# One transpose copy moved to ScalarE, the bias transpose planned later, new tie noise: a planned FFT-filter-and-MLP kernel on one core

## The chip, the core and the metric

One core of a Trainium2 chip runs the whole program. The metric is device time in microseconds (us) of one execution; a run's number is the median of several executions. Engines are named as in the profile: PE (TensorE) multiplies, PEld loads its weights, DVE is VectorE, ACT is ScalarE, POOL is GpSimd, SP is SyncE, which issues most DMAs.

## The reference, cut to what is computed

`x` is 2048 tokens of 512 values. A spectral branch filters it with a 2-D FFT, a dense branch is an MLP with the activation `h * tanh(softplus(h))` (Mish), and a gate per token mixes them.

```python
x = A_x                                                    # (1, 2048, 512) bf16
g = sigmoid((x * gate_w).sum(-1, keepdims=True))
a = irfft2(rfft2(x) * (A_w_r + 1j * A_w_i), s=(2048, 512)) # (2048, 257) filter
h = x @ B_w1 + B_b1                                        # 512 -> 1792
sp = log1p(exp(-abs(h))) + where(h > 0, h, 0)
b = (h * tanh(sp)) @ B_w2                                  # 1792 -> 512
return g * a + (1 - g) * b
```

## The kernel before, in words

**Tasks and a planner.** The kernel does not write its instruction order down. `_build` records 603 tasks with `G.add` and its wrappers (`pe`, `evict`, `tt`, `dma`; lines 449 to 487): each has an engine, a guessed duration, what it reads and writes, the banks of PSUM it needs and a priority. `_Graph.schedule` (line 203) then plays the program through with the guessed durations. At every step it takes the tasks that could start within 0.03 us of the earliest one and picks the one with the highest priority (lines 271 to 278). For loads the guess of when the data is there is a table, `LAND` (line 355). To each priority a small random number is added: `NOISE` times a draw from `SEED`, and for every number in `MORE` another 2% of the tasks draw again (lines 217 to 222). So ties, and near ties, are settled by the noise. What comes out is one fixed order per engine; the chip runs each engine's list strictly in that order, and a task waits on semaphores for those it depends on. Nothing is reordered at run time. Banks of PSUM are handed out by the planner too: a task that needs a bank waits for the one that last emptied it.

**Tiling.** Tokens are 16 tiles of 128. In what follows a task's name is that of the code:

- `tr0` to `tr3` (one tile each), `tr4`, `tr6` ... `tr14` (two each): PE transposes of x into PSUM, four 128x128 matmuls a tile (line 559). `evx0` ... copies the result to `xT` in SBUF (line 563, executed at lines 480 on DVE and 481 on ACT). Which engines may take a copy is said at line 565: tiles 8 to 15 DVE or ACT, the others DVE alone.
- The dense branch goes in four chunks of 512 tokens. `mm1_c_f` is chunk c times block f of 14 blocks of w1's columns: four matmuls of 128x512 into one bank (line 901). The first four blocks of chunk 0 are split into halves `a` and `b` of four 128x256 matmuls, since w1's rows land in two parts. `mish_c_f` (ACT, line 915) adds the bias `b1f` and applies Mish; it empties the bank. `mm2_t_0` and `mm2_t_1` are the two halves, seven matmuls each, of the second product for token tile t (line 932); `bev_t` (ACT, line 881) scales the result by 1-g for tiles 0 to 13, and `fin_14_1`, `fin_15_0` and `fin_15_1` (DVE, line 944) finish the last two.
- The bias: `ld_b1` loads b1 as 14 rows (ACT's DMA queue, line 529), `tr_small` turns it with one PE transpose (line 568), `ev_small` (DVE, line 571) writes `b1f`. Every `mish` needs it.
- The spectral branch, forward: `ts`/`td` add and subtract halves of `xT` (line 485, two of them on POOL); `a10_t`, `a11_t` (PE, line 597) are DFTs along the 512 values; `eg_t` (ACT, line 604) and `e1p_t`, `e1m_t`, `e1f_t` (DVE or ACT) combine them; `s1_t` (PE, line 628) is a first stage along the tokens; `e2_t` empties it and `r1w`/`r1r` DMAs reshape through memory. Then `s2_v0` (PE, line 736), the filter products `wm` (DVE, line 485, 128x1024) and `wz` (POOL, line 485, 128x510), and `s2i_v` (PE, line 819) back, with `e4` and a second pass through memory (`r2w`, `r2r`). A small side path corrects columns 0 and 256: `s2c` (PE, line 726), `cvec` (DVE, line 752), `crv` (POOL, lines 757 and 758), `rcc` (PE, lines 765 and 766), `cvec2`, `cm`, `chs`, `z0`.
- The spectral branch, last stage, per token tile t: `s1i_t` (PE, line 848), `e5_t` (DVE or ACT, lines 480 and 481), `a1i_t` (PE, line 860, into bank 5 or 6), `gc_t` (ACT, line 865), `sap_t` and `sam_t` (DVE, line 871), `sbp_t` and `sbm_t` (POOL, a few on DVE), and `sum_t` (DVE, line 485, 128x512), which adds the dense result before the store.
- The gate: `gdot_t` (DVE), `gpow` (POOL), then `gadd1` (line 655), `gcol1` (line 657) and `omg1` (line 658) on DVE for tiles 4 to 15.

Dense and spectral PE work has no order of its own but the data's: the planner fills the waits of the spectral chain with dense blocks. Before the first transposes PE runs 36 warm-up matmuls on constants (line 505).

The copy's options and the bias transpose, the places that the change touches:

```python
engs=("dve", "act") if t0 in EVA else ("dve",)             # EVA = (8, 10, 12, 14)
...
pe("tr_small", 0.1, ..., reads=["braw", "ident"], writes=["ptb"], alloc=pb)
```

Of the kernel before, what the change touches and what calls it, by code (L numbers as in the profile page):

```python
# [152 lines left out]
class _Graph:  # L153
# [49 lines left out]
    def schedule(self):  # L203
# [28 lines left out]
        while left:  # L232
# [100 lines left out]
S1N = 2  # L333
S1B = [(6, 7), (4, 5), (2, 3)]
A1B = (3, 4, 5)
SEED = 655
NOISE = 0.02
MORE = (875162, 119001, 117053, 53775, 256917, 33723, 661048, 937753, 617580, 523774, 550536, 317180, 864218, 698349, 47742, 135651, 44963, 55085, 378986, 311594, 322092, 969305, 898997, 781312, 307590, 286182, 632606)
SPEC = (3, 4, 5, 6, 7)
DENSE = {0: (0, 1), 1: (0, 1), 2: (0, 1, 7), 3: (0, 1, 7)}  # L340
DENSE2 = {0: (0, 1), 1: (0, 1), 2: (0, 1, 2, 7), 3: (0, 1, 2, 7)}
# [5 lines left out]
EVA = (8, 10, 12, 14)  # L347
GDD = 0
JOIN = 0
GD_N = 4  # L350
FOLDP = ('d2', 'd3')
P2B = ((2, 3), (4, 5))
PAIR = (0, 1, 2, 3)
COLD = 3.9
LAND = dict(ld_x0=3.0, ld_x1=3.2, ld_x2=4.0, ld_x3=4.3, ld_w1_a0=4.9, ld_w1_a1=5.1,
            ld_b1=6.3, ld_fd=6.3, ld_w1_b0=5.7, ld_w1_b1=6.1, ld_x4=9.0, ld_x6=9.2,
            ld_w1_4_0=10.0, ld_w1_4_1=10.6, ld_x8=12.0, ld_x12=13.6, ld_w1_8_0=14.4,
            ld_w1_8_1=15.1, ld_m10=16.6, ld_m11=17.9, ld_w1_12_0=18.4, ld_w1_12_1=18.8, ld_gw=19.2, ld_sm=19.5,
            ld_w2_0=22.0, ld_w2_1=24.4, ld_gd=24.8)
PR = dict(tr=99.0, sp=95.0, mm1=88.0, mish=97.0, mm2=70.0, fin=98.0, gate=96.9, sum=98.5)  # L360


def _build(nc, A_x, A_w_r, A_w_i, B_x, B_w1, B_b1, B_w2, gate_w, out):
# [6 lines left out]
    G = _Graph()  # L370
    es = ExitStack()
    with es:
# [4 lines left out]
        xT = sb("xT", [128, 4, NT * 128], BF)  # L377
        Tg = sb("Tg", [128, 8192], BF)
        act = sb("act", [128, 3, NFT, 512], BF)
# [5 lines left out]
        sm = sb("sm", [128, 320], BF)  # L385
# [31 lines left out]
        In2 = Abuf[:, 0:8192].rearrange("p (u g k) -> p u g k", u=8, g=4)  # L417
# [58 lines left out]
        def pe(name, dur, fn, **kw):  # L476
            return G.add(name, "pe", dur, fn, lat=0.17, **kw)
# [6 lines left out]
        def tt(name, o, i0, i1, op, n, rate=1.0, engs=("dve",), lock=True, **kw):  # L484
# [8 lines left out]
              reads=["ones"], writes=["ident"])  # L493
# [58 lines left out]
        for t0, w in ((0, 1), (1, 1), (2, 1), (3, 1), (4, 2), (6, 2), (8, 2), (10, 2), (12, 2), (14, 2)):  # L552
            pt = _Ps(SPEC[::-1])
            def f_tr(e, t0=t0, w=w, pt=pt):
                ins = None
                for i in range(w):
                    for c in range(4):
                        o, d0 = (c * w + i) * 128, 256 * (c // 2) + c % 2
                        ins = e.transpose(psb[:, pt.bank, o:o + 128], xo[:, t0 + i, d0:d0 + 255:2], ident[:, :])  # L559
                return ins  # L560

            pe(f"tr{t0}", 4 * w * mm(128), f_tr, reads=[("x", t0 + i) for i in range(w)] + ["ident"], writes=[("ptr", t0)], alloc=pt, prio=PR["tr"] + max(0, 4 - t0) * 0.2)
            evict(f"evx{t0}", 512 * w, lambda t0=t0, w=w: xT[:, :, 128 * t0:128 * (t0 + w)],
                  lambda pt=pt, w=w: psb[:, pt.bank, 0:512 * w].rearrange("p (c j) -> p c j", c=4), rate=2.0,
                  reads=[("ptr", t0)], writes=[("xT", t0 + i) for i in range(w)], frees=[pt], engs=("dve", "act") if t0 in EVA else ("dve",), prio=PR["tr"] + max(0, 4 - t0) * 0.2)
            if t0 == 3:
                pb = _Ps(SPEC[::-1])
                pe("tr_small", 0.1, lambda e, pb=pb: e.transpose(psb[:, pb.bank, 0:14].rearrange("p (a b) -> p a b", b=2), braw[0:14, :],
                                                                    ident[0:14, :].rearrange("p (b a) -> p a b", b=2)[:, 0:7, :]),
                   reads=["braw", "ident"], writes=["ptb"], alloc=pb)  # L570
                G.add("ev_small", "dve", 0.2, lambda e, pb=pb: e.tensor_copy(out=b1f[:, :], in_=psb[:, pb.bank, 0:14]),
                      reads=["ptb", "b1t"], writes=["b1f"], frees=[pb])
# [165 lines left out]
            return ins  # L738

        p2_01 = [[_Ps(P2B) for _ in range(2)] for _ in range(2)]  # L740
        if JOIN:

            def f_s2j(e):
                f_s2c(e)
                return f_s2(e, (0, 1), 2, p2_01[1])

            t_s20 = pe("s2_00", 2 * mm(512), lambda e: f_s2(e, (0, 1), 0, p2_01[0]), reads=[("In2", r, i) for r in range(2) for i in range(2)] + ["sm"],
                       writes=[("p2", 0, c) for c in range(2)], alloc=p2_01[0], prio=PR["sp"] + 1.6)
            pe("s2_cj", 0.03 + 2 * mm(512), f_s2j, reads=[("In2", r, u) for r in range(2) for u in range(8)] + ["sm"], writes=["pc", ("p2", 1, 0), ("p2", 1, 1)], alloc=[pc] + p2_01[1], deps=[t_s20], prio=PR["sp"] + 1.6)
        else:  # L750
            pe("s2c", 0.1, f_s2c, reads=[("In2", r, u) for r in range(2) for u in range(8)] + ["sm"], writes=["pc"], alloc=pc)
        G.add("cvec", "dve", 0.3, lambda e: e.tensor_copy(out=cvec[:, 0:2, :].rearrange("p c (r u) -> p r c u", r=2),
                                                          in_=ps[:, pc.bank:pc.bank + 2, 0:16].rearrange("p r (c u) -> p r c u", c=2)),
              reads=["pc"], writes=["cvec"], frees=[pc])
# [26 lines left out]
        for v in range(4):  # L781
            u0, zb = 2 * v, v % 2
            q_of = {}
            p2s = p2_01[v] if v < 2 and JOIN else [_Ps(P2B) for _ in range(2)]


            for cs in (((0, 1),) if v in PAIR else ((0,), (1,))):
                if v < 2 and JOIN:
                    continue
                pe(f"s2_{v}{cs[0]}", len(cs) * mm(512), lambda e, f=f_s2, cs=cs, u0=u0, p2s=p2s: f(e, cs, u0, p2s), reads=[("In2", r, u0 + i) for r in range(2) for i in range(2)] + ["sm"],  # L790
                   writes=[("p2", v, c) for c in cs], alloc=[p2s[c] for c in cs], deps=s2is[v - 2:v - 1] if v >= 2 else ())
            for c in range(2):
                p2 = p2s[c]
                for i in ((0, 1) if c == 0 else (1, 0)):
                    s = nq % 5
                    nq += 1
                    q_of[c, i] = s
                    tt(f"wm{v}{c}{i}", lambda s=s: Qb[:, s],
                       lambda p2=p2: ps[:, p2.bank:p2.bank + 2, :].rearrange("p r (u k) -> p r u k", u=2),
                       lambda i=i, u0=u0: WT[:, i, :, 0:256].rearrange("p (r u) k -> p r u k", r=2)[:, :, u0:u0 + 2, :],  # L800
                       ALU.mult, 1024, lock=False, reads=[("p2", v, c)] + WALL, writes=[("Q", s)], frees=[p2])
            for (c, k0, k1, op) in ((0, (0, 0), (1, 1), ALU.subtract), (1, (0, 1), (1, 0), ALU.add)):
                s0, s1 = q_of[k0], q_of[k1]
                for rho in range(2):
                    tt(f"wz{v}{c}{rho}", lambda zb=zb, c=c, rho=rho: Zb[:, zb, rho, c, :, 1:256],
                       lambda s0=s0, rho=rho: Qb[:, s0, rho, :, 1:256], lambda s1=s1, rho=rho: Qb[:, s1, rho, :, 1:256], op, 510,
                       engs=("pool",), reads=[("Q", s0), ("Q", s1)], writes=[("Z", zb, rho, c)])
            G.add(f"wc{v}", "pool", 0.2, lambda e, zb=zb, u0=u0: e.tensor_copy(
                out=Zb[:, zb, :, :, :, 0], in_=z0[:].rearrange("p c (r u) -> p r c u", r=2)[:, :, :, u0:u0 + 2]),
                reads=["z0"], writes=[("Z", zb, 2)], lock=True)  # L810
            p3 = _Ps([(4, 5, 6, 7)])

            def f_s2i(e, zb=zb, p3=p3):
                ins = None
                for c in range(2):
                    for rho in range(2):
                        for g in range(4):
                            r = slice(32 * g, 32 * g + 32)
                            ins = e.matmul(ps[64 * rho:64 * rho + 64, p3.bank + g, :], RI[r, c, :],  # L819
                                           Zb[r, zb, rho, c].rearrange("p u k -> p (u k)"), start=(c == 0), stop=(c == 1))  # L820
                return ins

            t_s2i = pe(f"s2i_{v}", 2 * mm(512) + 0.04, f_s2i, reads=[("Z", zb, 2)] + [("Z", zb, r, c) for c in range(2) for r in range(2)] + ["sm"],
               writes=[("p3", v)], alloc=p3)
            s2is.append(t_s2i)
            for g2 in range(2):
                evict(f"e4_{v}{g2}", 1024, lambda u0=u0, g2=g2: T2s[:, u0:u0 + 2, 2 * g2:2 * g2 + 2, :].rearrange("p u g k -> p g u k"),
                      lambda p3=p3, g2=g2: ps[:, p3.bank + 2 * g2:p3.bank + 2 * g2 + 2, :].rearrange("p g (u k) -> p g u k", u=2),
                      reads=[("p3", v)] + S1R, writes=[("T2s", v, g2)], frees=[p3])
            dma(f"r2w{v}", scr2_w[:, 8 * v:8 * v + 8, :], T2s[:, u0:u0 + 2].rearrange("p u g k -> p (u g) k"),  # L830
                reads=[("T2s", v, 0), ("T2s", v, 1)], writes=[("scr2", v)], nbytes=128 * 4096, tail=0.5)
# [235 lines left out]
```

## Time and profile before

| | before |
|---|---|
| median of 3 runs | 131.83 us (131.78 to 131.84) |
| the profiled execution, its own time | 131.52 us |
| its span, first to last instruction | 129.8 us |
| TensorE clock granted | 1.00 |
| PE busy | 126.1 us, 97% of the span |
| DVE, ACT, POOL busy | 90.5, 73.4, 62.8 us |

Busy time is the time in which an engine executed; a row of the timeline gives its start, its length, engine, line, operation and tiles (out<-in) and how many instructions of the kind it merges; in brackets stands idle time of that engine ahead of it, with what ended it. The ends of PE's matmuls are modelled, so two PE rows may overlap by some tenths; starts are what counts.

### The profile page before, as it was taken

Reading aid. Unit: us, or ns where it says so; the run is one execution under the profiler, and the core shown is the slowest. Engines: PE = TensorE matmul, PEld = TensorE weight load, DVE = VectorE, ACT = ScalarE, POOL = GpSimd, SP = SyncE. Lnnn points to the kernel's source line nnn. Section 1 sums busy time; section 2 is a strip of 40 time slices with the busy share of each in tenths; the row PEclk is TensorE's granted clock in tenths of the full one; section 3 lists DMA queues with packets and bytes.
Section 4 is the critical chain, followed back from the end, with each engine's and each line's share of the span. In section 5 each row is a group of like instructions: output and inputs, shape, how many; then the busy total and the mean of one; then the engine's idle time right before and its main releaser. Section 6 shows DMA issues by size and latency. Waiting matters only on the chain. (4 is left out here: it accounts for less than half of the span.)

```text
span 129.8 us, 2596 instructions
## 1 busy us (share of the span) xinstructions
PE 126.1 (97%) x983; PEld 67.0 (52%) x983; DVE 90.5 (70%) x166; ACT 73.4 (57%) x120; POOL 62.8 (48%) x90
## 2 busy tenths in 40 slices
PE   7899999999999999999999999999999999999992
PEld 7787756454544443433343434344566555545452
DVE  0538989997669978978694863300267998999672
ACT  0456779755642776768678688804357374362230
POOL 3000143993536025976979094000019689579700
PEclk9999999999999999999999999999999999999999
DMA  3999999699995494800410503156910022222024
GB/s 93 304 355 400 384 343 333 203 221 228 204 319 167 94 374 188 323 5 0 127 37 0 162 5 107 54 162 197 408 47 3 0 86 81 81 83 81 0 87 160
DMA packets 15929, 21.11 MB, mean 163 GB/s; under 512 B 1324, under 2 KB 12588, under 8 KB 15532
## 3 DMA queue, kind: packets, MB, share of 16 engines
q1 hardware_dynamic: 14112, 16.63, 38.2%
q0 software_dynamic: 768, 3.15, 9.7%
q10 hardware_dynamic: 1036, 1.15, 2.8%
q8 instruction: 8, 0.13, 0.4%
q14 instruction: 5, 0.04, 0.1%
HBM read 14.64 MB, written 6.29 MB: 161 GB/s over the span
## 5 line engine op out<-in xcount | busy, mean ns | idle before, releaser
L901 PE MATMUL ps<-xT,w_sb 128*128 128x512 bf16 (+1 forms) x240 | 52.1, 365 | 0.2 <-DVE xT L480 0.2
L932 PE MATMUL ps<-w_sb,act 128*128 128x512 bf16 (+2 forms) x238 | 51.9, 366 | 0.0
L915 ACT ACTIVATE act<-ps,b1f 128x512 bf16<-128x512 f32 x56 | 38.4, 687 | 15.2 <-PE ps L901 14.2
L901 PEld LDWEIGHTS ps<-xT,w_sb 128*128 128x128 bf16 x240 | 22.0, 98 | 24.5 <-issue 3.3
L932 PEld LDWEIGHTS ps<-w_sb,act 128*128 128x128 bf16 x238 | 21.8, 98 | 21.2 <-issue 0.2
L485 POOL TENSOR_TENSOR Tg<-Qb 128x256 bf16<-128x256 f32 x29 | 21.4, 769 | 21.7 <-DVE Qb L871 21.7
L485 POOL TENSOR_TENSOR Zb<-Qb 128x510 bf16<-128x510 f32 x16 | 19.9, 1267 | 6.2 <-DVE Qb L485 6.2
L485 DVE TENSOR_TENSOR Qb<-ps,WT 128x1024 f32<-128x1024 f32 x16 | 18.6, 1215 | 4.5 <-PE ps L736 4.5
L881 ACT ACTIVATE xo<-ps,omg 128x512 bf16<-128x512 f32 x14 | 9.6, 687 | 19.1 <-PE ps L932 18.8
L480 DVE CAST Ybuf<-ps 128x1024 bf16<-128x1024 f32 x8 | 9.8, 1223 | 9.7 <-PE ps L819 6.6
L871 DVE SCALAR_TENSOR_TENSOR Qb<-ps,gcol,Qb 128x256 f32<-128x256 f32 x32 | 13.8, 473 | 1.8 <-ACT Qb L865 0.9
L480 DVE CAST Zb<-ps 128x512 bf16<-128x512 f32 x8 | 5.4, 685 | 11.6 <-PE ps L848 11.6
L485 POOL TENSOR_TENSOR Tg<-xT 128x1024 bf16<-128x1024 bf16 x2 | 4.2, 2122 | 17.5 <-DVE xT L480 13.8
L485 DVE TENSOR_TENSOR Abuf<-ps,Tg 128x512 bf16<-128x512 f32 x16 | 10.3, 683 | 2.8 <-ACT Tg L604 2.2
L865 ACT ACTIVATE Qb<-ps,gcol 128x256 f32<-128x256 f32 x16 | 7.4, 471 | 7.1 <-PE ps L860 7.1
L646 DVE SCALAR_TENSOR_TENSOR Tg<-xo,Tg 128x512 bf16<-128x512 bf16 x16 | 11.0, 688 | 0.5
L481 ACT ACTIVATE Ybuf<-ps 128x1024 bf16<-128x1024 f32 x8 | 8.2, 1023 | 3.6 <-PE ps L628 3.6
L485 DVE TENSOR_TENSOR xo<-xo,Tg 128x512 bf16<-128x512 bf16 x14 | 9.2, 689 | 0.4 <-ACT xo L881 0.4
L480 DVE COPY xT<-ps 128x1024 bf16<-128x1024 bf16 (+1 forms) x9 | 4.8, 566 | 5.2 <-PE ps L559 5.2
L450 POOL DMA_DIRECT2D scr<-Ybuf x8 | 5.3, 662 | 4.8 <-ACT Ybuf L481 4.8
L653 POOL TENSOR_TENSOR gcol<-omg,gdot 128x4 f32<-128x4 f32 (+1 forms) x2 | 3.4, 1681 | 6.5 <-DVE Tg L646 6.5
L860 PE MATMUL ps<-GDs,Zb 128*128 128x128 bf16 x64 | 6.2, 219 | 0.1
(69 smaller groups left out, 90.8 us busy)
## 6 DMA issues: line engine op xcount, KB each, us to landing
Abuf<-scr SPq DMA_DIRECT2D x8, 512.0 KB, 5.4
scr<-Ybuf SPq DMA_DIRECT2D x4, 512.0 KB, 3.2
w_sb<-in_B_w_dram SPq DMA_DIRECT2D x2, 896.0 KB, 11.6
out_dram<-xo SPq DMA_DIRECT2D x6, 256.0 KB, 2.0
WT<-in_A_w_r_dram POOLq DMA_DIRECT2D x4, 257.0 KB, 5.0
WT<-in_A_w_i_dram POOLq DMA_DIRECT2D x4, 257.0 KB, 7.9
w_sb<-in_B_w_dram SPq DMA_DIRECT2D x4, 256.0 KB, 7.5
xo<-in_A_x_dram SPq DMA_DIRECT2D x2, 512.0 KB, 7.7
```

The source lines that it names most:

```text
L450: t = G.add(name, queue, issue, lambda e: e.dma_start(dst, src), reads=reads, writes=writes, lat=tail, deps=deps, prio=prio)
L480: fs = {"dve": ("dve", dve_dur(n, rate=rate), lambda e: e.tensor_copy(out=dst(), in_=src())), "act": ("act", act_dur(n), lambda e: e.activ ...
L481: "act": ("act", act_dur(n), lambda e: e.activation(dst(), src(), AF.Copy))}
L485: f = lambda e: e.tensor_tensor(out=o(), in0=i0(), in1=i1(), op=op)
L646: lambda e, t=t: e.scalar_tensor_tensor(out=junk, in0=xo[:, t, :], scalar=1.0, in1=gwb, op0=ALU.mult, op1=ALU.mult, accum_out=gdot[:, t:t ...
L860: ins = e.matmul(ps[:, p5.bank, 128 * i:128 * i + 128], TT[:, sl, 2 * par + ri, :], GDs[:, i, :], start=True, stop=True)
L865: lambda e, t=t, sl=sl, p5=p5: e.activation(gC[:, sl, :].rearrange("p (i n) -> p i n", i=2), ps[:, p5.bank, :].rearrange("p (i n) -> p i n ...
L871: lambda e, t=t, sl=sl, p5=p5, o=o, op=op: e.scalar_tensor_tensor(out=st1[:, sl, o::2, :], in0=ps[:, p5.bank, :].rearrange("p (i n) -> p i ...
L881: G.add_multi(f"bev_{t}", [("act", act_dur(512, True), lambda e: e.activation(xo[:, t, :], ps[:, pd.bank, :], AF.Copy, scale=omg[:, t:t + ...
L901: ins = e.matmul(ps[:, pd.bank, j:j + w], w1_sb[:, i, 128 * ft:128 * (ft + 1)], xT[:, i, 512 * c + j:512 * c + j + w], start=(i == 0 and j ...
L915: lambda e, ft=ft, pd=pd, hb=hb: e.activation(act[:, hb, ft, :].rearrange("p (t a b) -> p t a b", t=4, b=2), ps[:, pd.bank, :].rearrange(" ...
L932: ins = e.matmul(ps[:, pd.bank, cs_], act[:, hb, ft, 128 * tl:128 * (tl + 1)], w2_sb[:, ft, cs_], start=(ft == 0), stop=(ft == NFT - 1))
```

## The change

Four edits, of which one only tidies:

- `evx2`, the copy of token tile 2's transposes, may go to ACT alone. `evx0`, `evx1` and `evx3` stay on DVE.
- `LAND` says that b1 lands at 7.1 instead of 6.3 and the DFT table `FD` at 6.4 instead of 6.3. These are the planner's guesses; the loads themselves, their queues and their order are as before.
- `SEED` is another number and `MORE` has 18 other numbers instead of 27.
- `JOIN`, which is 0 before and after, is now asked `JOIN == 1`, and a branch for `JOIN == 2` is added. With 0 none of it is taken.

```diff
-SEED = 655
+SEED = 300570
...
-            ld_b1=6.3, ld_fd=6.3, ld_w1_b0=5.7, ld_w1_b1=6.1, ld_x4=9.0, ld_x6=9.2,
+            ld_b1=7.1, ld_fd=6.4, ld_w1_b0=5.7, ld_w1_b1=6.1, ld_x4=9.0, ld_x6=9.2,
...
-                  reads=[("ptr", t0)], writes=[("xT", t0 + i) for i in range(w)], frees=[pt], engs=("dve", "act") if t0 in EVA else ("dve",), prio=PR["tr"] + max(0, 4 - t0) * 0.2)
+                  reads=[("ptr", t0)], writes=[("xT", t0 + i) for i in range(w)], frees=[pt], engs=("act",) if t0 == 2 else ("dve", "act") if t0 in EVA else ("dve",), prio=PR["tr"] + max(0, 4 - t0) * 0.2)
...
-        if JOIN:
+        if JOIN == 1:
```

Both kernels have the same 603 tasks. What the edits do to the planned order, read from the two programs:

| engine | what moves |
|---|---|
| PE, start | `tr_small` stood after `mm1_0_1a`; now after `mm1_0_0a`, `1a`, `0b`, `1b` and `a10_0` |
| PE, up to `mm1_1_0` | DFT, first-stage and dense blocks change places in many spots; `mm2` halves of tiles 0 to 3 in another order |
| PE, `mm1_1_0` to `mm1_3_13` | the same order |
| PE, last stage | `s1i`, `a1i` and `mm2` halves interleaved in another order; the last two, `mm2_15_0` and `mm2_15_1`, as before |
| ACT | `evx2` after the table-loading activation and before `eg_0`; later `eg`, `e1f`, `e2`, `bev`, `gc`, `e5` in another order |
| DVE | `evx3` right after `evx1`; `gadd1` straight after `wm000` (before: after `wm010`), `cvec` after `omg1` (before: ahead of it); many swaps in the last stage |
| POOL | small swaps among `wz`, `wc`, `sbp`, `sbm`; `sbp_15` from DVE to POOL |
| SP | the same order |

In the last stage, PE's order around the two places that the prediction speaks of:

```
before: ... mm2_8_0 s1i_8 a1i_6 s1i_9 mm2_8_1 s1i_10 a1i_5 mm2_10_0 ...
after:  ... mm2_8_0 a1i_6 s1i_8 a1i_4 s1i_10 mm2_10_1 s1i_9 mm2_8_1 a1i_5 a1i_7 s1i_11 mm2_9_0 ...
before: ... mm2_10_1 a1i_11 mm2_13_0 a1i_12 mm2_14_0 a1i_13 mm2_14_1 a1i_15 ...
after:  ... mm2_13_0 a1i_11 mm2_12_0 a1i_12 mm2_12_1 a1i_13 mm2_14_0 a1i_15 ...
```

More of the change, by code (lines that the diff above doesn't have):

```diff
@@ L335 @@
 A1B = (3, 4, 5)
-SEED = 655
+SEED = 300570
 NOISE = 0.02
-MORE = (875162, 119001, 117053, 53775, 256917, 33723, 661048, 937753, 617580, 523774, 550536, 317180, 864218, 698349, 47742, 135651, 44963, 55085, 378986, 311594, 322092, 969305, 898997, 781312, 307590, 286182, 632606)
+MORE = (754822, 886038, 820155, 228879, 497271, 805584, 735615, 584617, 895747, 837205, 524683, 517246, 95632, 592802, 64915, 997243, 725492, 342141)
 SPEC = (3, 4, 5, 6, 7)
@@ L750, in _build @@
         else:
-            pe("s2c", 0.1, f_s2c, reads=[("In2", r, u) for r in range(2) for u in range(8)] + ["sm"], writes=["pc"], alloc=pc)
+            t_s2c = pe("s2c", 0.1, f_s2c, reads=[("In2", r, u) for r in range(2) for u in range(8)] + ["sm"], writes=["pc"], alloc=pc)
         G.add("cvec", "dve", 0.3, lambda e: e.tensor_copy(out=cvec[:, 0:2, :].rearrange("p c (r u) -> p r c u", r=2),
@@ L783, in _build @@
             q_of = {}
-            p2s = p2_01[v] if v < 2 and JOIN else [_Ps(P2B) for _ in range(2)]
+            p2s = p2_01[v] if v < 2 and JOIN == 1 else [_Ps(P2B) for _ in range(2)]
             for cs in (((0, 1),) if v in PAIR else ((0,), (1,))):
-                if v < 2 and JOIN:
+                if v < 2 and JOIN == 1:
                     continue
@@ L801, in _build @@
                        ALU.mult, 1024, lock=False, reads=[("p2", v, c)] + WALL, writes=[("Q", s)], frees=[p2])
+                    if v == 0 and JOIN == 2:
+                        t_s2c.deps.append(G.tasks[-1])
             for (c, k0, k1, op) in ((0, (0, 0), (1, 1), ALU.subtract), (1, (0, 1), (1, 0), ALU.add)):
```

## The prediction, as put on record before the changed kernel ran

> **What bounds the kernel now.** I read the page's busy times first, then PE by stage, then the timeline at PE's start and wherever PE waits.
>
> ```profile
> PE 126.1 (97%) x983; PEld 67.0 (52%) x983; DVE 90.5 (70%) x166; ACT 73.4 (57%) x120; POOL 62.8 (48%) x90
> ...
> 0.00:6.15 6.15, 4.87 (x52) 4.47 (x53) 1.53 (x5) 1.49 (x2) 1.18 (x10) 1.00 0.63 189
> 6.15:42.40 36.25, 36.17 (x312) 21.64 (x312) 29.17 (x62) 21.90 (x38) 16.07 (x25) 1.00 0.95 287
> 42.40:83.47 41.07, 41.07 (x312) 16.66 (x311) 29.77 (x41) 31.37 (x45) 24.08 (x26) 1.00 0.35 116
> 83.47:127.50 44.03, 43.94 (x311) 24.27 (x309) 29.63 (x60) 18.62 (x36) 21.42 (x29) 1.00 0.30 105
> ```
>
> The first line is the page's; the others are stretches of the span (length, then busy time of PE, PEld, DVE, ACT, POOL). From the first dense block at 6.15 to 127.5 PE is never seen idle for long. So only three things change the time: when PE's dense work begins, the short waits inside, and the 2.3 us behind the last matmul. PE's work itself does not change. The start:
>
> ```profile
> 3.77 1.28 ACT L499 ACT_TABLE_LOAD   x1 [3.77 <-issue]
> 5.06 0.20 ACT L499 ACTIVATE b1f<-b1f 128x1 f32<-128x1 f32 x1
> 5.19 0.39 PE L559 MATMUL ps<-ident,xo 128*128 128x128 bf16 x4
> 5.34 0.76 DVE L480 COPY xT<-ps 128x512 bf16<-128x512 bf16 x2 [0.24 <-PE ps L559]
> 6.15 1.05 PE L901 MATMUL ps<-xT,w_sb 128*128 128x256 bf16 x8 [0.22 <-DVE xT L480]
> 7.28 0.09 PEld L568 LDWEIGHTS ps<-ident,braw 14*128 14x128 bf16 x1 [0.36 <-DMA braw<-in_B_b_dram]
> 7.28 0.18 PE L568 MATMUL ps<-ident,braw 14*128 14x14 bf16 x1
> 7.39 1.05 PE L901 MATMUL ps<-xT,w_sb 128*128 128x256 bf16 x8
> ```
>
> DVE copies tiles 2 and 3 one behind the other, 5.34 to 6.10; the dense block follows 0.05 later. Then the bias transpose stops PE until 7.28, because b1 has not landed. In the last stage PE waits twice for DVE (line 871, `sap`/`sam`, which empty the bank of `a1i`):
>
> ```profile
> 104.10 0.23 PEld L860 LDWEIGHTS ps<-GDs,Zb 128*128 128x128 bf16 x4 [0.23 <-DVE Qb L871]
> 104.11 0.40 PE L860 MATMUL ps<-GDs,Zb 128*128 128x128 bf16 x4
> ...
> 115.83 0.23 PEld L860 LDWEIGHTS ps<-GDs,Zb 128*128 128x128 bf16 x4 [0.52 <-DVE Qb L871]
> 115.83 0.40 PE L860 MATMUL ps<-GDs,Zb 128*128 128x128 bf16 x4
> ```
>
> Starts give the size: `s1i_10` at 103.66 takes 0.22 as every quartet, so `a1i_5` at 104.11 waited 0.23. The seven matmuls ahead of `a1i_12` begin at 114.13 and take 1.51, so 115.83 is 0.19 late.
>
> **1. Tile 2 on ACT.** Removed: one DVE copy ahead of tile 3's. A copy alone takes 0.42 (mean of line 480's 128x512 group, 418 ns). Tile 3's matmuls end at 5.19 + 0.39 = 5.58; a copy starts 0.04 behind (5.30 to 5.34 for tile 2), so tile 3 is copied 5.62 to 6.04 instead of to 6.10. Added: one ACT copy; line 604's activations of the same shape take 592 ns, ACT is free at 5.26 and tile 2 is ready at 5.34: 5.34 to 5.93, beside DVE. The later end, 6.04, decides, and the first block starts at about 6.10: **0.05 won**. ACT has 0.11 to spare; the whole of line 481's 128x1024 copy (1023 ns) would end at 6.36 and lose 0.27, half of it would end at 5.85. I take 592, the nearest row. The add and subtract of chunk 0 wait for both copies and start 0.05 earlier, too.
>
> **2. The bias transpose later.** In the old place: eight matmuls (two half blocks) take 8.28 - 7.39 = 0.89, so PE could have gone on at 7.04; the switch to a small shape costs 0.10 where nothing waits (`s2c`, due at 49.09 + 5 x 0.865 = 53.42, starts at 53.52). 7.28 - 7.04 - 0.10 leaves **0.14 of waiting, which goes**: in the new order PE gets there at 6.10 + 4 x 0.44 + 0.22 = 8.08, long after 7.28. What is late next: w1's second part landed at 6.87 (ACT's issue at 2.20, 4.67 to landing) and is now wanted at 6.10 + 0.88 = 6.98: it fits by 0.1. The first DFT wants DVE's add and subtract, which end 5.62 + 0.42 + 0.04 + 1.29 = 7.37, against 7.86. Behind the transpose, `ev_small` ends at about 8.5; ACT meanwhile does `eg_0` (8.3 to 8.9), so the first Mish starts at 8.8 instead of 8.04. Its bank is wanted by `mm1_0_3a` at 9.8: Mish ends at 9.5. The wait of 0.08 at `mm1_0_5` for `mish_0_3` (PE comes back to its bank one block later) stays.
>
> **3. The noise, up to 42.40.** I walked the new order with these starts and durations. Every quartet, block and shape change occurs as often as before, so PE's length is the same if nothing is late. The closest places: Mish to the block that reuses its bank, 0.13 (0.04 + 0.69 + 0.06 of hand-over against 0.86 + 0.22 of PE work between); `s1_8` behind `eg_12`, 0.26; DFT `a11_8` behind DVE's `e2_0`, 0.34; `mm2_1_0` behind the last Mish, 0.14. None is negative. Transfers keep their queues and order on SP and ACT; POOL's `td3` comes 2 us earlier, so POOL reaches its filter loads as soon as w2 has landed (24.44) instead of 24.95. Cost: nothing, covered by dense blocks; a miss at one of them costs its excess.
>
> **4. The noise, 42.40 to 83.47.** PE's order is unchanged and its waits there have 0.24 or more to spare, so it moves as a whole, the reloads from memory (`s2_00` had 1.5, `s1i_1` 1.2 to spare) with it. Changed is the gate's place on DVE:
>
> ```profile
> 51.67 3.76 POOL L485 TENSOR_TENSOR Zb<-Qb 128x510 bf16<-128x510 f32 x3 [1.45 <-DVE Qb L485]
> 52.64 0.32 DVE L655 TENSOR_SCALAR omg<-gcol 128x12 f32<-128x12 f32 x1
> 54.26 1.21 DVE L658 TENSOR_SCALAR omg<-gcol 128x12 f32<-128x12 f32 x1
> ```
>
> Line 658 needs 0.17 alone (32.28, POOL idle) but took 1.21 and ended with POOL's product (51.67 + 3.76 = 55.43). `gadd1` now comes straight behind `wm000`, at 51.52, and POOL's first product at 51.67 (released by `wm000`). If DVE is first: nothing. If POOL is, `gadd1` ends at 52.96, `wm010` 1.2 later than I count, `wz010` at 56.7, `crv` at 57.1, and `rcc` (56.95) waits **0.2**. I take nothing, as DVE starts 0.15 sooner, and keep 0.2 for the range.
>
> The Trainium skill (SBUF — State Buffer, "SBUF: two separate sides") calls the port pair of DVE and GpSimd an exclusive lock held for the whole instruction by whoever starts first. The 1.21 agrees. By that rule nothing is shared: either `gadd1` comes first and the sum below stays at 0.61, or POOL does and it is 0.41; that is why A has more than a small chance.
>
> **5. The noise, last stage.** Times unshifted, from 83.47. `a1i_5` now stands behind two `mm2` halves: PE comes at 105.39. Its bank needs `sap_4`: DVE does the same three sums (101.11, 2.15 with POOL beside) and one more product (0.39) ahead of it and ends at 104.45. **0.23 goes.** `a1i_12` at 116.90 needs `sam_9`, which follows `a1i_9` (113.64), a cast (0.61), `gc_9` and two products: about 115.5. **0.19 goes.** Next closest: `a1i_13` behind `sap_11`, 0.39 if both sums ahead of it take 0.95 (POOL busy) instead of 0.42; `a1i_4` behind `sap_3`, 0.45. The end: the last products, `fin_15_0` and the store stay 2.3 us behind PE; DVE's earlier work ends about 0.5 ahead of `fin_15_0`, as now (0.47 idle).
>
> **6. `JOIN`, `LAND`:** no instruction; nothing.
>
> **Sum.** 0.05 + 0.14 + 0.23 + 0.19 = 0.61 off the span of 129.8. The profiled execution took 131.52, so 130.91; the runs' median is 0.31 above that execution, so **131.2**.
>
> **Rivals.**
> A. *A new short wait takes part of it* (`gadd1` as in 4, or one of the places in 3): 0.2 to 0.3 back, 131.45. For: margins of 0.13 and guesses of 0.1. Against: PE-to-ACT hand-over was 0.04 in every row.
> B. *The last stage keeps its waits elsewhere.* DVE is busy 29.6 of 44 there; if its sums always meet POOL (0.95), `a1i_13` or `a1i_14` waits. Only the start is won: 131.65.
> C. *Slower: DVE falls behind in the last stage.* Place: `a1i`'s two banks, emptied by `sap`/`sam`. Price: one for one beyond 0.4 of lag; three more sums at 0.95 than I count are 1.6, so 1.2 of waiting against 0.61 won: 132.4. It decides from a lag of 1.0. Against: `sum` rows of 0.42 and 0.95 are about half and half before.
> D. *Slower: ACT is not free at 5.26.* The copy is late from 5.44 on, one for one. If what follows the table load lasts as long again (1.28), the copy ends at 7.13 and the first block starts at 7.19: 1.04 lost against 0.14 + 0.42 still won: 132.3. Against: the activation starts 0.01 behind the load, and one load (x1) serves all Mish and copies.
> The Trainium skill (ScalarE: Activation LUTs, "What ACT_TABLE_LOAD costs") states a drain of about 1.38 us on top of 1.28; by it the copy would start at 6.43, the first block at 7.1 and the time would be an estimated 132.2. The row at 5.06 speaks against it.
> E. *The orders balance out*, several small waits I did not see: 131.8. That the change does nothing is excluded: the changed program has the copy on ACT and the new orders.
>
> **Chances.** Forecast 0.58; A 0.16; B 0.09; E 0.07; C 0.07; D 0.03. 0.2% is 0.26 us, about what a measurement of this kernel can tell from no change: A counts as faster, B lies beside the line (0.18 gained: same). Faster 0.74, same 0.16, slower 0.10. The range goes from 130.9 (rounding of the starts, 0.1 to 0.2, and the 0.08 at `mm1_0_5`, all to the good) to 131.9: above it lie C and D, a tenth, and below it less.
>
> **What would show it.** In the profile after: line 901 starts at 6.10, not 6.15 (step 1); ACT has a 128x512 copy of `xT` of 0.59 ending before DVE's; no idle `<-DMA braw` (2); `mm1_1_0` at 42.2 (3); line 655 at 0.16, not 0.3 to 1.4 (4); no `<-DVE Qb L871` ahead of line 860 (5); last matmul 0.6 earlier. I am wrong if ACT's copy starts after 5.45, or if PE shows idle behind `mish`, `eg` or `sap` anywhere new.

## The result, and the profile after

Six runs each, side by side: 131.06 us after (130.82 to 131.36) against 131.81 before (131.71 to 132.01), ratio 0.9943 with a 95% interval of 0.9928 to 0.9959. The prediction said 131.2. The profiled execution took 130.82 us with a span of 129.1, against 131.52 and 129.8 before. Lines from 802 on are three higher than before: 901 is now 904, 860 is 863, 871 is 874.

The page's busy times, then the same four stretches as in the prediction, cut at the same events:

```profile
PE 125.7 (97%) x983; PEld 67.4 (52%) x983; DVE 88.1 (68%) x165; ACT 74.2 (57%) x120; POOL 63.9 (49%) x91
```

```profile
0.00:6.05 6.05, 4.97 (x53) 4.58 (x53) 1.27 (x4) 2.04 (x3) 1.19 (x10) 1.00 0.67 194
6.05:42.14 36.09, 36.09 (x312) 21.86 (x312) 29.59 (x65) 22.05 (x37) 16.09 (x25) 1.00 0.96 288
42.14:83.20 41.06, 41.06 (x311) 16.65 (x310) 27.92 (x39) 31.43 (x45) 24.04 (x26) 1.00 0.36 116
83.20:126.80 43.60, 43.60 (x311) 24.36 (x309) 29.00 (x59) 18.66 (x36) 22.54 (x30) 1.00 0.30 106
```

The lengths say where the time went: 0.10 in the start (6.15 to 6.05), 0.16 up to `mm1_1_0` (36.25 to 36.09), 0.01 in the middle, 0.43 in the last stage (44.03 to 43.60). The sum is the 0.70 between the spans. The start, from the timeline (the row at 4.79 is `tr2`, the one at 5.09 `tr3`):

```profile
3.78 1.28 ACT L499 ACT_TABLE_LOAD   x1 [3.78 <-issue]
4.79 0.23 PEld L559 LDWEIGHTS ps<-ident,xo 128*128 128x128 bf16 x4 [0.20 <-DMA xo<-in_A_x_dram]
5.07 0.21 ACT L499 ACTIVATE b1f<-b1f 128x1 f32<-128x1 f32 x1
5.09 0.39 PE L559 MATMUL ps<-ident,xo 128*128 128x128 bf16 x4
5.23 0.60 ACT L481 ACTIVATE xT<-ps 128x512 bf16<-128x512 bf16 x1
5.51 0.42 DVE L480 COPY xT<-ps 128x512 bf16<-128x512 bf16 x1 [0.39 <-PE ps L559]
6.05 1.91 PE L904 MATMUL ps<-xT,w_sb 128*128 128x256 bf16 x16 [0.23 <-DVE xT L480]
8.11 0.18 PE L568 MATMUL ps<-ident,braw 14*128 14x14 bf16 x1
```

ACT copies tile 2 (0.60 us) while DVE waits for tile 3 and copies it alone, to 5.94. Sixteen matmuls of line 904 run on without a break, and the bias transpose (line 568) comes behind them with no wait. But the first block begins 0.11 behind DVE's copy, where it was 0.06 before. Something else held it; the experiments show what. And `tr2`, which waits for x2 to land, had begun 0.10 later in the profile of before:

```profile
4.90 0.23 PEld L559 LDWEIGHTS ps<-ident,xo 128*128 128x128 bf16 x4 [0.40 <-DMA xo<-in_A_x_dram]
```

The gate's rows, from the timelines of DVE and POOL:

```profile
51.25 0.16 DVE L655 TENSOR_SCALAR omg<-gcol 128x12 f32<-128x12 f32 x1
...
51.41 3.72 POOL L485 TENSOR_TENSOR Zb<-Qb 128x510 bf16<-128x510 f32 x3 [2.17 <-DVE omg L655]
...
53.66 0.27 DVE L658 TENSOR_SCALAR omg<-gcol 128x12 f32<-128x12 f32 x1
```

`gadd1` is at 0.16, and POOL's first product starts at 51.41, just as `gadd1` ends. That is 0.08 behind the end of `wm000` (51.33), as it was before (51.59 to 51.67), so nothing shows that one held the other; the bracket names the last DVE instruction that had ended. `omg1`, 1.21 before, now takes 0.27 and ends at 53.93, about when POOL's second product does (three take 3.72 from 51.41 on, so 53.89). The rule of the Trainium skill (SBUF — State Buffer, "SBUF: two separate sides") that whoever starts first keeps the shared port for its whole instruction agrees with the row of `omg1`. The row of `gadd1` does not test it. The last stage:

```profile
103.62 1.67 PE L935 MATMUL ps<-w_sb,act 128*128 128x512 bf16 x7
...
105.13 0.61 PE L863 MATMUL ps<-GDs,Zb 128*128 128x128 bf16 x8
...
115.14 1.67 PE L935 MATMUL ps<-w_sb,act 128*128 128x512 bf16 x7
...
116.65 0.39 PE L863 MATMUL ps<-GDs,Zb 128*128 128x128 bf16 x4
```

`a1i_5` (105.13) and `a1i_12` (116.65) start 1.51 behind the seven matmuls ahead of them, which is what seven take: no wait, no bracket.

### The profile page after: what moved, and what is told of

Its sections match the earlier page's. It is cut to its first block, busy times and chain, and to the rows that moved or that the text cites. A ratio compares the mean times of both kernels' runs of the same rounds, so it can differ in the third digit from the quotient of the medians.

```text
span 129.1 us, 2591 instructions
## 1 busy us (share of the span) xinstructions
PE 125.7 (97%) x983; PEld 67.4 (52%) x983; DVE 88.1 (68%) x165; ACT 74.2 (57%) x120; POOL 63.9 (49%) x91
## 3 DMA queue, kind: packets, MB, share of 16 engines
q10 hardware_dynamic: 1036, 1.15, 2.9%
HBM read 14.64 MB, written 6.29 MB: 162 GB/s over the span
## 4 chain that ended last, share of the span: by engine, by line
PE 97%; DVE 1%; issue 0%
PE ps L904 38%; PE ps L935 38%; PE ps L559 3%; PE ps L597 3%; PE ps L628 3%; PE ps L863 3%; PE ps L851 3%; PE ps L505 2%; PE ps L822 2%; PE ps L736 2%; DVE xT L480 0%; DVE xo L947 0%; PE ps L726 0%; PE ps L568 0%; PE ps L676 0%
## 5 line engine op out<-in xcount | busy, mean ns | idle before, releaser
L485 POOL TENSOR_TENSOR Tg<-Qb 128x256 bf16<-128x256 f32 x30 | 22.5, 777 | 22.1 <-DVE Qb L874 22.1
L485 DVE TENSOR_TENSOR xo<-xo,Tg 128x512 bf16<-128x512 bf16 x14 | 8.5, 640 | 0.0
L604 ACT ACTIVATE Tg<-ps 128x512 f32<-128x512 f32 x8 | 4.6, 594 | 3.3 <-PE ps L597 3.3
```

Of the source, the lines that this page charges most:

```text
L485: f = lambda e: e.tensor_tensor(out=o(), in0=i0(), in1=i1(), op=op)
L604: G.add(f"eg_{t}", "act", act_dur(512), lambda e, gb=gb, pa=pas[0], pv=pv: e.activation(G0[:, gb].rearrange("p t c (m s) -> p t c m s", s= ...
```

## Experiments

**How they are read.** The runs of one kernel scatter by 0.2 to 1.4 us, as much as the effects. So each profile is also cut at three events: the start of the first dense block, the first `s1i`, and the start of the last matmul. The last stretch repeats to 0.01 where the order is the same; the one ahead of it differs by single waits of up to 0.15, named below. What comes after the last matmul is 2.5 in all. (In four profiles 15 or 16 of PE's 983 records are missing; the three events are not among them. The lengths are differences of starts read to 0.01.) Medians are of 6 to 12 runs; before beside them gave 131.72 (first four), 131.79 (next four) and 131.79 (last four).

| kernel | median | ratio to before | block starts | block to `s1i` | `s1i` to last matmul |
|---|---|---|---|---|---|
| before | 131.81 | 1 | 6.15 | 86.38 | 34.76 |
| after | 131.06 | 0.9943 (0.9928 to 0.9959) | 6.05 | 86.22 | 34.32 |
| e1 new start, old end | 131.58 | 0.9987 (0.9966 to 1.0007) | 6.17 | 86.34 | 34.76 |
| e2 old start, new end | 131.26 | 0.9961 (0.9940 to 0.9981) | 6.48 | 86.26 | 34.32 |
| e3 copy only | 131.81 | 1.0002 (0.9982 to 1.0023) | 6.94 | 86.22 | 34.76 |
| e4 bias only | 131.87 | 1.0007 (0.9988 to 1.0026) | 6.60 | 86.35 | 34.76 |
| e5 two quartets only | 132.52 | 1.0054 (1.0038 to 1.0070) | 6.44 | 86.22 | 35.65 |
| e6 after, bias early | 131.06 | 0.9949 (0.9930 to 0.9968) | 6.23 | 86.23 | 34.32 |
| e7 after, copy on DVE | 131.10 | 0.9953 (0.9935 to 0.9971) | 6.04 | 86.37 | 34.32 |
| e8 after, two moves more | 130.91 | 0.9938 (0.9915 to 0.9961) | 7.15 | 86.00 | 34.32 |
| e9 e5 with a slot | 132.63 | 1.0074 (1.0053 to 1.0095) | 6.54 | 86.23 | 35.63 |
| e10 e9 with sums moved | 132.25 | 1.0046 (1.0026 to 1.0066) | 6.41 | 86.33 | 35.40 |
| e11 as e8 | 130.75 | 0.9925 (0.9903 to 0.9946) | 6.26 | 86.02 | 34.32 |
| e12 as after | 131.18 | 0.9964 (0.9945 to 0.9984) | 6.45 | 86.23 | 34.32 |

**e1, e2: which half of the order.** Both use two draws of noise: the tasks of the last stage take one kernel's `SEED` and `MORE`, all others the other's. e1 is the changed kernel with the old draw for the last stage, e2 the kernel before with the new draw there.

```diff
-        noise = np.random.RandomState(SEED).uniform(-1, 1, len(tasks))
...
+        late = np.array([_late(t.name) for t in tasks])
+        noise = np.where(late, draw(SEED2, MORE2), draw(SEED, MORE))
```

> Everything of the change up to the last stage (copy on ScalarE, later bias transpose, new noise), but the last stage planned with the old noise, so its order is that of before. My theory (the terms are separate waits of TensorE and add up): the two waits of line 863 (a1i_5 and a1i_12, 0.23 and 0.19) are back, the start's 0.2 to 0.26 stays won: 131.55. Rival (the gain is one thing, an earlier start that everything behind rides on, and the waits of the last stage only looked separate): most of the 0.75 stays, 131.2 or less.

> The kernel before, with the last stage alone planned with the new noise. My theory: no wait at a1i, 0.42 to 0.44 won, 131.38; the first dense block at 6.15 and the wait for b1 as before. Rival (the start carries the gain): 131.7.

The last stage is 34.76 with the old draw and 34.32 with the new one, whatever the start is: the 0.44 belongs to the orders of that stage alone. In e1's timeline both waits for DVE are back (its lines are 13 higher than in the changed kernel):

```profile
104.08 0.23 PEld L876 LDWEIGHTS ps<-GDs,Zb 128*128 128x128 bf16 x4 [0.23 <-DVE Qb L887]
...
115.80 0.23 PEld L876 LDWEIGHTS ps<-GDs,Zb 128*128 128x128 bf16 x4 [0.52 <-DVE Qb L887]
```

The medians agree: e2 is 0.46 below before beside it, with an interval clear of 1; e1 is 0.14 below, with an interval that holds 1. Of e2's forecast the time came true and the start did not: its first block came at 6.48, and the bias transpose did not wait.

**e3, e4: one edit of the start alone.** The kernel before, its planned order edited: in e3 `evx2` goes to ACT behind the table's activation; in e4 `tr_small` goes behind `a10_0`.

```diff
+        order["dve"].remove(ev)
+        ev.eng, ev.fn = "act", ...                       # e3
+        order["act"].insert(... behind "table", ev)
...
+        put("pe", "tr_small", "a10_0")                   # e4
+        put("act", "eg_0", "table")
```

> The kernel before with the copy of tile 2 alone moved to ScalarE, behind the table load; every other order as before. My theory as predicted: tile 3's copy ends 0.05 earlier and so does the first dense block, 131.76, below what the times can tell, so the trace decides: from the start of tile 3's transposes to the first dense block 0.91 instead of 0.96. Rival, from the trace of after, where that distance is 0.96 as before: the copy gains nothing, since the hand-over to TensorE grew from 0.06 to 0.11 (one semaphore more to wait for) or since w1 lands only then: 0.96 again.

> The kernel before with the bias transpose alone moved behind a10_0 on TensorE, and eg_0 ahead of the first Mish on ScalarE, as in after. My theory: the wait for b1 (0.14) goes and nothing else comes late: 131.67; no idle time of TensorE ended by the DMA of braw, mm1_1_0 0.14 earlier than before. Rival: the bank that the first Mish empties, or the DFT stage behind a later eg_0, gives it back: 131.8, with a new wait of TensorE between 9 and 20 us.

Neither moves the median (the intervals hold 1, half a width 0.2%). e3's first block starts late, at 6.94: w1's first part landed at 6.81 in that run, while the copies had ended at 6.36. So this profile cannot tell 0.91 from 0.96, the question that it was to settle. In e4 the wait for b1 is gone, but a wait of 0.11 comes at `mm1_0_3a`: Mish starts later behind the later bias, and has not emptied the bank when PE comes back to it. With the rest of the new order there is no such wait.

**e6, e7: one edit of the start taken back from the changed kernel.** e6 puts `tr_small` back behind `mm1_0_1a`; e7 puts `evx2` back on DVE behind `evx1`.

```diff
+        put("pe", "tr_small", "mm1_0_1a")                # e6
...
+        order["act"].remove(ev)                          # e7
+        ev.eng, ev.fn = "dve", ...
+        order["dve"].insert(... behind "evx1", ev)
```

> The changed kernel with the bias transpose put back behind mm1_0_1a. My theory: the wait for b1 is back, 0.14, TensorE idle until about 7.28: 131.2. Rival (in the new order the wait is hidden, or the first Mish comes earlier and pays for it): 131.06.

> The changed kernel with tile 2 copied by VectorE again. As predicted: the first dense block 0.05 later, 131.11. Rival (the copy gained nothing): 131.06, and from the start of tile 3's transposes to the first dense block 0.96 as with the copy on ScalarE. The times alone cannot tell the two apart; the trace can.

Both medians are those of the changed kernel within 0.04. Cut at events, each edit has a size, but not one that a median shows:

- *The copy.* From the start of tile 3's transposes to the end of its copy it takes 0.90 to 0.91 with both copies on DVE (before, e5, e7) and 0.84 to 0.85 with ACT's help (after, e1, e6, e8, e11, e12): 0.05 to 0.06 won. This needs transposes at their full rate. In e2, e3 and e4 tile 3's matmuls still started 107 ns apart, and it took 1.10 with both copies on DVE (e2, e4) and 1.09 with ACT's help (e3): tile 2 was copied before tile 3 was ready, and nothing was won. (In e9 and e10 the rate changed in the midst of the transposes of tiles 2 and 3.) And the block also needs w1's first part. In all 14 profiles, the last four taken after the rule was written down, it starts at the later of two times, within 0.02: the copy's end + 0.06, and that part's landing + 0.14. The copy decides in before, e1, e2, e4, e6, e7, e9, e10; w1 decides in after (landed 5.91), e3 (6.81), e5 (6.30), e8 (7.01) and e12 (6.32); in e11 both give 6.26. In e12's timeline ACT and DVE are done at 5.88, and PE waits on:

```profile
5.18 0.60 ACT L481 ACTIVATE xT<-ps 128x512 bf16<-128x512 bf16 x1
...
5.46 0.42 DVE L480 COPY xT<-ps 128x512 bf16<-128x512 bf16 x1 [0.35 <-PE ps L559]
...
6.45 1.91 PE L904 MATMUL ps<-xT,w_sb 128*128 128x256 bf16 x16 [0.68 <-DMA w_sb<-in_B_w_dram]
```

- *The bias.* With the early place the transpose follows 0.96 to 1.00 behind the first block's start where b1 has landed. It took 1.13 in before and 1.07 in e10, and 0.96 to 1.00 in e2, e3, e5, e6 and e9: a wait of 0.15 or 0.09 in two of seven profiles, none in five. Which it is follows from b1's landing, the last update of its semaphore in the trace: 6.60 to 7.82 in the 14 profiles. PE goes on 0.05 behind it (7.23 to 7.28 in before, 7.43 to 7.48 in e10), so the early place waits where the landing is later than the block's start + 0.93; all seven profiles fit. By the same two times the early place would also have waited in e1 (0.28) and e4 (0.13) and in none of the other five. Over the 14 that is 0.05 on average, an estimate of what the later place is worth.
- *e7's 0.15 between block and `s1i`* is neither: the first `s1` starts at 17.78, 0.14 behind the landing of its table's first part (17.64; in after that part landed at 16.98).

**e5, e9, e10: is it only where the two quartets stand?** e5 is the kernel before with `a1i_5` moved behind `mm2_10_0` and `a1i_12` behind `mm2_14_0`.

```diff
+        put("pe", "a1i_5", "mm2_10_0")
+        put("pe", "a1i_12", "mm2_14_0")
```

> The kernel before with two quartets of the last stage moved one half block later on TensorE (a1i_5 behind mm2_10_0, a1i_12 behind mm2_14_0), nothing else. My theory: those two waits for VectorE are all that the new noise took away in the last stage; both go, 0.42 won: 131.4. Rival (the whole order of VectorE matters, the two waits are only where its lag shows): the lag shows at another quartet, 131.6 to 131.8, with a new wait at line 860.

It is slower than either theory said: the last stage takes 35.65. The two old waits (0.42) are gone, and 1.3 of new ones has come. The largest, in its timeline:

```profile
105.52 0.61 PE L860 MATMUL ps<-GDs,Zb 128*128 128x128 bf16 x8
...
105.94 0.69 DVE L480 CAST Zb<-ps 128x512 bf16<-128x512 f32 x1 [0.98 <-PE ps L860]
...
106.69 0.74 PE L848 MATMUL ps<-m1g,Abuf 128*128 128x128 bf16 x8 [0.56 <-DVE Zb L480]
```

`e5_9` writes the slot of `TT` (four slots, tile modulo 4) that `a1i_5` reads. With `a1i_5` later DVE idles 0.98, and `s1i_11`, which needs the bank that `e5_9` empties, comes 0.73 late; `s1i_13` another 0.13, `a1i_9` 0.23. e9 gives tile 9 a fifth slot. e10 also moves `sum_3` ahead of `sam_5` and `sum_4` behind `sam_7`.

```diff
+            ts = 4 if t == 9 else sl                     # e9, e10
...
+        put("dve", "sum_3", "e5_9")                      # e10
+        put("dve", "sum_4", "sam_7")
```

> As the run with a1i_5 and a1i_12 moved alone, but tile 9's cast e5_9 writes a fifth slot, so it need not wait until a1i_5 has read slot 1. Stretch from the first s1i to the last matmul: 34.76 before, 34.32 after, 35.65 with the two moves alone, which had new waits of 0.73 (s1i_11, for e5_9), 0.13 (s1i_13), 0.23 (a1i_9), 0.06 and 0.17 (near 120 and 122). Theory 'the slot': the cast's wait was all; 0.73 and 0.13 go, the stretch is about 34.8 and the time that of before. Theory 'the whole order of VectorE': sam_5 still waits for gc_5, which follows the moved a1i_5 (about 106.4), and two sums stand between it and sam_7, which ends at 109.4 as in the run before; so the 0.73 goes and a1i_9 waits about 1.0 in place of 0.23: stretch still about 35.6, time about 0.7 above before.

> As the run with the fifth slot, and two sums moved on VectorE: sum_3 ahead of sam_5 (into the gap until gc_5), sum_4 behind sam_7. Theory 'the whole order of VectorE': sam_7 ends at about 108.2, so a1i_9 (due at 108.4) no longer waits; only the 0.06 and 0.17 near the end stay: stretch from the first s1i to the last matmul 34.6, that is 0.2 below before and 0.25 above after. Theory 'the slot': the sums change nothing against the run with the slot alone, whatever that gave.

Neither theory held in e9. The stretch stays at 35.63, as the second theory said, but that is luck: `a1i_9` waits only 0.21, not 1.0, and the large wait is elsewhere:

```profile
105.00 0.68 DVE L480 CAST Zb<-ps 128x512 bf16<-128x512 f32 x1
...
105.63 0.61 PE L861 MATMUL ps<-GDs,Zb 128*128 128x128 bf16 x8
...
106.06 0.47 ACT L866 ACTIVATE Qb<-ps,gcol 128x256 f32<-128x256 f32 x1 [1.27 <-PE ps L861]
...
106.43 0.59 ACT L481 ACTIVATE Zb<-ps 128x512 bf16<-128x512 f32 x1
...
107.16 0.38 PE L849 MATMUL ps<-m1g,Abuf 128*128 128x128 bf16 x4 [0.70 <-ACT Zb L481]
```

The cast no longer waits (105.00) and `s1i_11` is in time. But on ACT `gc_5` stands ahead of `e5_10`; it waits for `a1i_5` (idle 1.27), so `e5_10` comes at 106.43 and `s1i_13`, which needs its bank, is 0.86 late. That is e5's 0.73 + 0.13: behind the slot stood ACT's order, with the same end. e10's sums take away the 0.21 at `a1i_9` as forecast and leave the 0.86, so the stretch is 35.40 where 34.6 was forecast. In the changed kernel's timeline ACT runs `e5_10` right behind `e5_8`, ahead of `gc_5`, and a half block stands between `s1i_11` and `s1i_12`. So the two moves on PE do not give the gain by themselves; e2 shows that the last stage's orders, all engines together, do. That PE, DVE and ACT each have a part is argued from these waits. Which of the many other swaps are needed was not tried.

**e8, e11, e12: a version that beats both.** e8 and e11 are the changed kernel with two moves: tile 8's transposes ahead of `mm1_0_5`, where PE waits 0.08 for a bank, and `s2c` next to `s2_10`, which has the same tile shape. e12 is the changed kernel.

```diff
+        put("pe", "tr8", "mm1_0_4")
+        put("pe", "s2c", "mm1_1_10")
```

> The changed kernel with two more moves on TensorE: tr8 ahead of mm1_0_5, whose wait of 0.08 for a bank it would cover, and s2c right ahead of s2_10, so that one change of the array's shape in and out (0.09 + 0.10, the second shown behind s2c) is shared. My theory: 0.08 + 0.19 won, 130.8. Rival: the correction path behind s2c (cvec, crv, rcc), now 1.7 us later, makes rcc or mm1_2_4 wait, and the 0.19 or more is lost: 131.0 or slower.

> The changed kernel with tile 8's transposes ahead of the fifth dense block and s2c ahead of s2_10, beside the changed kernel itself on the same chip. By the traces its stretch from the first dense block to the last matmul is 120.32 against 120.54: 0.2 faster than the changed kernel, 0.9 faster than before. Rival: the small wait near 54 and the later transposes take it back in most runs, and the two are the same within 0.1.

> The changed kernel itself, for the comparison on one chip: about 0.75 below before. Its profile shows which of two things starts the first dense block: tile 3's copy (its end + 0.06) or w1's first part (its landing + 0.14). The start is then the later of the two, within 0.02; the rival is that the copy decides in every run.

From the first block to the last matmul it takes 120.32 and 120.34 against 120.54 and 120.55: 0.21 to 0.22 of the 0.27 that was forecast for e8. On one chip e11's runs lie at 130.64 to 130.84 and e12's at 130.74 to 131.95; the medians are 0.43 apart. 0.2 of that is shown by the stretches; the rest is within what the start scatters. e12's start is the w1 landing + 0.13, not the copy's end + 0.06 (5.94): the rule of the later of two held.

## Why the prediction was right, step by step

1. *Tile 2 on ACT, 0.05:* the size was right (0.05 to 0.06) where the transposes run at their full rate, and so were ACT's start and length (5.23, 0.60 for 592 ns). What the step left out is a second input: w1's first part, which in before was ready at 5.84 + 0.14 = 5.98, only 0.17 ahead of the copy. In the profile after it decided (6.05), and 6.05 is also what DVE alone would have given (5.09 + 0.90 + 0.06). So the 0.10 by which that profile starts earlier is x2's landing (4.75 for 4.86), a matter of the run: `tr2` started 0.05 behind it and `tr3` 0.29 behind `tr2` in both. The copy won nothing there.
2. *The bias transpose, 0.14:* it is there in the profile of before (1.13 against some 0.98) and gone after. But it is a wait of that execution, not of the kernel: two of seven profiles with the early place show it, and 0.05 is the estimate over 14 landings. The step mis-sized the term for the median by reading it from one profile. "It fits by 0.1" for w1's second part was also too wide, since w1's landing reaches PE 0.14 later: in e1 the part landed at 7.02, and PE waited 0.10 until 7.15.
3. *Noise up to 42.40:* nothing was late, and the 0.08 at `mm1_0_5` stayed. `mm1_1_0` is at 42.14 (forecast 42.2). The margin of 0.13 for Mish does not follow from the numbers in its bracket, which leave 0.29 (1.08 less 0.79).
4. *Gate:* DVE came first, `gadd1` at 0.16; no price.
5. *Last stage, 0.42:* 0.44, shown by e1 and e2. In e1 the two waits are 0.23 and 0.19 again, 0.42 of it. The step rested on the whole new order of DVE; e5 shows that the two moves on PE alone cost 0.9. Rival C's place, `a1i`'s banks and DVE's lag, was a real danger and not the only one: e9 adds `s1i`'s banks and ACT's order.
6. *The sum:* 0.61 forecast, 0.70 in the profiles; the difference is x2's landing (0.10, where 0.05 stood for the copy) and hundredths. What is left for the kernel is 0.44 for certain, some 0.05 for the bias (0 to 0.28 by the run) and 0 to 0.06 for the copy, some 0.5 on average. e2's 0.46 fits that. The changed kernel's 0.61 and 0.75 against before lie above it, with intervals of 0.21 to 0.72 and 0.54 to 0.95: that the first median came so close to the forecast is in part luck, since the bias had been taken as 0.14 and a single profile's start as the kernel's.

## What to carry to other kernels

Cut profiles at events that both kernels share: stretches that repeat to a few hundredths tell 0.2 us apart where medians cannot, and they show which terms belong to the run. Before a faster producer is credited, list every other input of its consumer with its time of arrival and its hand-over. And where lists run strictly in order, an instruction that is moved alone holds up what other engines have queued behind its result: walk every engine's list, not only the one that waits.

## What the runs showed of the hardware

- w1's first part reached PE 0.13 to 0.14 after its landing (7.01 to 7.15, 6.81 to 6.94, 6.30 to 6.44, 6.32 to 6.45), and so did the first `s1`'s table (17.64 to 17.78). x2 and b1 reached it after 0.05 (4.86 to 4.90 and 7.23 to 7.28 in before). Why the two differ is open. A DVE copy reached PE after 0.05 to 0.06. The same load of w1 landed between 5.68 and 7.01 in 14 executions.
- PE's matmuls of 128 columns start 107 ns apart at first and 56 ns apart later, and the change comes at another time in each execution: the last slow one ended between 3.56 (e1, e12) and 6.29 (e2). The trace's record of the granted clock agrees: it says 1.00 from 3.75 (e12) to 6.56 (e2) on and nothing of the time ahead (e3 and e4 have no record), so the 1.00 in the start's row does not show this. In e2 and e4 the transposes of tiles 2 and 3 still ran slowly, and from tile 3's transposes to the first block it took 1.15 instead of 0.96. The Trainium skill (TensorE: Matmul & The Clock Gate, "What's actually happening") gives a free-running window of some 3.4 us as the reason and +-500 ns as the spread; the spread of 2.7 seen here is wider than that, though shorter than the window.
